# Linear attention followed by a gated MLP, one core: early loads on two hardware queues, ss a pair later between zero matmuls, and batch 1's q transposed by TensorE

## The chip, the cores and the metric

The kernel runs on one core of a Trainium2 chip. The metric is the device time of one execution in microseconds. A kernel's time is the median of several runs.

## The reference

Eight batches of eight heads, 576 positions, head width 64, all in float32. Attention has no softmax: per head a 64x64 matrix is built from k and v, q is multiplied by it, and each row is normalised by its root mean square and scaled by `g_norm`. The heads are put side by side (4608 rows of 512), and a two-layer MLP with a sigmoid-approximated GELU follows.

```python
kv = np.einsum('bhsd,bhse->bhde', k, v)
out = np.einsum('bhsd,bhde->bhse', q, kv)
rms = np.sqrt(np.mean(out * out, axis=-1, keepdims=True) + 1e-06)
attn_out = out / rms * g_norm                      # 8, 8, 576, 64
x = attn_out.transpose(0, 2, 1, 3).reshape(4608, 512)
h = x @ moe_w_in                                   # 512 -> 2048
g = h * (1.0 / (1.0 + np.exp(-1.702 * h)))
out = g @ moe_w_out                                # 2048 -> 512
```

## The kernel before

All matmuls are in float16 with float32 sums. Heads are handled in four pairs (`c` = 0 to 3), two heads of 64 side by side on 128 partitions. For a pair, attention is: `kv` (the pair's 64x64 matrices, copied to `kvb`), a transposed q (`qT`), `out` (one matmul of `kvb` with `qT`, then a square `sq` on ScalarE), `ss` (a matmul with ones that sums the squares over a head, then `ln` and `rs` on ScalarE) and `apply` (VectorE multiplies the out tile by `g_col` and `rs` into `xT`). 512 of the 576 rows of a batch go through its own dense block; the last 64 of all batches are gathered in `x_rem` for a ninth block.

`dense(t, ...)` is the MLP for 512 rows: 16 hidden tiles `hT` of four matmuls each with `w_in_sb`, a gate on ScalarE into `gT`, and 64 projection steps with `w_out_sb` into four `o` tiles, which are copied to `osb` and stored. Blocks 0 and 1 start with a group of four hidden tiles, for which the outer loop runs over the four parts `ko` of x. In block 0 the projection goes through the weights in four quarters (`deep`). Work of the next batch's attention is put between the matmuls of a block by two tables: `at1(i, f)` runs f after hidden tile i (or ahead of part i of the group), `at2(n, f)` after projection step n. Each engine executes in the order in which the code is written.

Batches 0 and 1 are loaded with 96 partitions of 6 rows each (`PE_`, `NJ`), the other batches with 128 partitions of 4 rows, whole and early by `load_batch`. Loads that GpSimd issues (`early_load`, `load_w_in`, `load_w_out`) go through one software queue and cast to float16 on the way; SyncE's and ScalarE's go through hardware queues and do not cast. Batch 0 (`First`): q and k of pairs 0 and 1 come by SyncE as float32 (`first`) and are cast by ScalarE and VectorE, everything else of it by GpSimd. Its q is transposed by TensorE through `ident` (12 transposes a pair). Batch 1 (`Second`): its q, k and v are packed into `qbuf` and `kbuf` by VectorE, and q is transposed by one DMA (`qTe`) that SyncE issues. Batches 2 to 7 use DMA transposes too (`qTd`, `qTr`). Batch 2's load is issued by `third`, which waits until `w_out` is complete.

Ahead of and between batch 0's matmuls stand zero matmuls: `busy(n)` multiplies a cleared tile n times into `idle_ps`, which nothing reads.

PSUM is divided into three pools: `ps_a` ("att", three buffers: out, ss, kvp), `ps_h` ("hT", three) and `ps_o` ("o", two).

Of the kernel before, what the change touches and what calls it, by code (L numbers as in the profile page):

```python
# [7 lines left out]
F16 = mybir.dt.float16  # L8
F32 = mybir.dt.float32
# [3 lines left out]
P = 128  # L13
# [3 lines left out]
def kernel(  # L17
# [10 lines left out]
    nc = tc.nc  # L28

    B, H, S, D = q.shape  # L30
    DM = H * D
    DFF = moe_w_in.shape[1]
    NPAIR = H // 2
# [3 lines left out]
    SM = 512  # L37
# [5 lines left out]
    PE_ = 96  # L43
    NJ = S // PE_
# [37 lines left out]
    def early_src(n, b, c0, c1):  # L82
        return srcs[n][b, 2 * c0 : 2 * c1].rearrange("h (p j) d -> p h (j d)", j=NJ)

    def early_load(n, b, c0, c1):
        nc.gpsimd.dma_start(
            out=raw[n][0:PE_, c0:c1, :].rearrange("p c (l x) -> p (c l) x", l=2),
            in_=early_src(n, b, c0, c1),
        )

    def pack(n, dst, c):

        nc.vector.tensor_copy(  # L93
            out=dst[0:PE_, c * NJ * P : (c + 1) * NJ * P].rearrange(
                "p (j l d) -> p j l d", j=NJ, l=2
            ),
            in_=raw[n][0:PE_, c, :].rearrange("p (l j d) -> p j l d", l=2, j=NJ),
        )
# [37 lines left out]
            nc.gpsimd.tensor_copy(out=t.rearrange("p c (l d) -> p (c l) d", l=2), in_=src[n])  # L136


    HW = 2
    first = {}  # L140
    for n in "qk":
        first[n] = stage.tile([P, H, J * D], F32, name=f"{n}f", tag=f"{n}f")
        first[n] = first[n].rearrange("p h x -> p (h x)")[0:PE_, 0 : HW * 2 * NJ * D]
        first[n] = first[n].rearrange("p (c x) -> p c x", c=HW)
    for c in range(HW):
        for n in "qk":
            nc.sync.dma_start(  # L147
                out=first[n][:, c, :].rearrange("p (h x) -> p h x", h=2),
                in_=early_src(n, 0, c, c + 1),
            )  # L150
    g_row = const.tile([1, D], F32)
    nc.scalar.dma_start(out=g_row, in_=g_norm.unsqueeze(0))
    nc.vector.memset(ident, 0.0)
    nc.vector.memset(kvb[1], 0.0)
    for c in range(HW):
        early_load("v", 0, c, c + 1)
    nc.gpsimd.affine_select(
        out=ident,
        in_=ident,
# [3 lines left out]
        pattern=[[-1, P]],  # L163
        channel_multiplier=1,
    )
    for c in range(HW, NPAIR):
        for n in "qkv":
            early_load(n, 0, c, c + 1)

    nc.scalar.preload_act_table_set("natural_log_exp_and_others")  # L170
# [8 lines left out]
    def load_w_in(f0, f1):  # L179
        nc.gpsimd.dma_start(  # L180
            out=w_in_sb[:, :, f0 * P : f1 * P],
            in_=moe_w_in[:, f0 * P : f1 * P].rearrange("(ko ki) f -> ki ko f", ki=P),
        )
# [8 lines left out]
    xT = {}  # L192

    class Attention:
        def __init__(self, b):
            self.b, self.kb = b, kvb[b % 2]
            self.qT, self.o = {}, {}
            self.x = xT[b] = xpool.tile([P, KO, SM], F16, name="xT", tag="xT")
# [23 lines left out]
        def transpose_q(self):  # L222
            s = attn.tile([P, NPAIR * J, P], F16, name="qTd", tag="qTd", bufs=1)
            nc.sync.dma_start_transpose(out=s, in_=qbuf[:, 0 : NPAIR * SM])
            self.qTr = attn.tile([P, 2, P], F16, name="qTr", tag="qTr", bufs=1)
            nc.sync.dma_start_transpose(
                out=self.qTr, in_=qrem[self.b % 2].rearrange("p c e -> p (c e)")
            )
            s = s.rearrange("p (c j) r -> p c (j r)", c=NPAIR)
            for c in range(NPAIR):  # L230
                self.qT[c] = s[:, c, :]
# [30 lines left out]
        def ss(self, c, table=False):  # L262
            if table:
                nc.scalar.preload_act_table_set("natural_log_exp_and_others")  # L264
            o, sq, n = self.o[c]
            t = ps_a.tile([P, SM], F32, name="ss", tag="att")
            nc.tensor.matmul(t[:, 0:n], ones2, sq[:, 0:n], start=True, stop=True)  # L267
            ln = attn.tile([P, SM], F32, name="ln", tag="ln", bufs=2)
            nc.scalar.activation(ln[:, 0:n], t[:, 0:n], AFT.Ln, bias=eps_t, scale=1.0 / D)  # L269
            rs = attn.tile([P, SM], F32, name="rs", tag="rs", bufs=2)  # L270
            nc.scalar.activation(rs[:, 0:n], ln[:, 0:n], AFT.Exp, bias=0.0, scale=-0.5)  # L271
            self.o[c] = (o, rs, n)
# [16 lines left out]

    class First(Attention):  # L290


        def kv(self, c):
            t = ps_o.tile([P, D], F32, name="kv0", tag="o")
# [16 lines left out]
        def q(self, c):  # L311
            t = ps_h.tile([P, S], F16, name="q0", tag="hT")
            for j in range(NJ):
                for hl in range(2):
                    nc.tensor.transpose(
                        t[hl * D : (hl + 1) * D, j * PE_ : (j + 1) * PE_],
                        qraw[0:PE_, c, (hl * NJ + j) * D : (hl * NJ + j + 1) * D],
                        ident[0:PE_, 0:PE_],
                    )
            s = attn.tile([P, S], F16, name="qT", tag="qT", bufs=4)  # L320
            nc.vector.tensor_copy(s, t)
            self.qT[c] = s
# [4 lines left out]
    class Second(Attention):  # L327


        def pack_q(self):  # L330
            for c in range(NPAIR):
                pack("q", qbuf, c)

        def pack_k(self, c):
            pack("k", kbuf, c)
# [14 lines left out]
            if c == NPAIR - 1:  # L350
                self.keep_kv()

        def transpose_q(self):
            s = attn.tile([P, NPAIR * NJ, PE_], F16, name="qTe", tag="qTe", bufs=1)
            nc.sync.dma_start_transpose(out=s, in_=qbuf[0:PE_, :])
            s = s.rearrange("p (c j) r -> p c (j r)", c=NPAIR)
            for c in range(NPAIR):
                self.qT[c] = s[:, c, 0:SM]
            self.qTe = s

        def rest(self, c):
            return self.qTe[:, c, SM:S]


    def dense(t, units1, units2, group, deep):
# [88 lines left out]

    a0 = First(0)

    def first_cast(c):
        nc.scalar.copy(qraw[0:PE_, c, :], first["q"][:, c, :])
        nc.vector.tensor_copy(kraw[0:PE_, c, :], first["k"][:, c, :])


    idle_ps = ps_h.tile([P, SM], F32, name="idle", tag="hT")
# [1 line left out]
    def busy(n):  # L464
        for _ in range(n):
            nc.tensor.matmul(
                idle_ps,
                kvb[1][:, 0, :],
                kvb[1].rearrange("p c r -> p (c r)"),
                start=True,  # L470
                stop=True,
            )

    first_cast(0)
    busy(8)
    g_ps = ps_o.tile([P, 1], F32, name="g_ps", tag="o")
    for hl in range(2):
        r = slice(hl * D, (hl + 1) * D)
        nc.tensor.matmul(g_ps[r, :], g_row, one_t, start=True, stop=True)
    nc.vector.tensor_copy(g_col, g_ps)  # L480
    a0.q(0)
    busy(6)
    first_cast(1)
    for c in range(NPAIR):
        last = c == NPAIR - 1
        a0.kv(c)
        if not last:
            a0.q(c + 1)
            if c:
                a0.apply(c - 1)  # L490
        a0.out(c)
        if last:
            a0.apply(c - 1)
        else:
            a0.ss(c)
            busy(1)
    load_w_in(0, 4)
    load_w_in(4, 8)
    load_w_in(8, 16)
# [20 lines left out]
    for t in range(NT):  # L520
        b = t + 1
        u1, u2 = {}, {}

        def at1(i, f, *args):
            u1.setdefault(i, []).append(lambda: f(*args))

        def at2(i, f, *args):
            u2.setdefault(i, []).append(lambda: f(*args))

        def of(b, name, *args):  # L530
            return lambda: getattr(live[b], name)(*args)

        if t == 0:
            at1(("ko", 1), of(0, "ss", NPAIR - 1))
            at1(("ko", 1), of(0, "apply", NPAIR - 1))
            at1(4, of(0, "out", NPAIR))
            at2(4, of(0, "ss", NPAIR, True))
            at2(4, of(0, "apply", NPAIR))
            at1(8, start, 1)
            for r in krem + vrem:  # L540
                at1(8, nc.vector.memset, r[R:P], 0.0)
            at1(12, of(1, "pack_q"))
            at1(12, of(1, "transpose_q"))
            for c in range(NPAIR):
                at2(12, of(1, "pack_k", c))
                at2(23 + c, of(1, "kv", c))
                at2(30 + 8 * c, of(1, "out", c))
                at2(38 + 8 * c, of(1, "ss", c))
                at2(38 + 8 * c, of(1, "apply", c))
            at2(14, third)  # L550
        elif b < B:
            if t == 1:
                at2(46, of(1, "out", NPAIR))
                at2(53, of(1, "ss", NPAIR))
                at2(53, of(1, "apply", NPAIR))
            f0 = 7 if t == 1 else 2
            at1(f0, casts, b)
            at1(f0, start, b)
            at1(f0, of(b, "transpose_q"))
            if t == 1:  # L560
                at1(f0, load_batch, 3)
            for c in range(NPAIR):
                at1((11 if t == 1 else 9) + c, of(b, "kv", c))
            for c in range(NPAIR + 1):
                at2(1 + 9 * c, of(b, "out", c))
                at2(8 + 9 * c, of(b, "ss", c, c == 0))
                at2(8 + 9 * c, of(b, "apply", c))
            if b + 2 < B:
                at2(2, load_batch, b + 2)
        dense(t, u1, u2, 4 if t < 2 else 0, t == 0)  # L570
# [30 lines left out]
```

## Time and profile before

| | before |
|---|---|
| median of 3 runs | 305.53 us (305.33 to 306.51) |
| profiled execution, its own time | 305.53 us |
| span of the profile | 303.7 us |
| granted TensorE clock, mean | 0.967 |
| TensorE busy | 289.4 us (95%), 1517 matmuls |
| ScalarE busy | 176.4 us (58%) |
| VectorE busy | 89.1 us (29%) |
| software queue | 7.14 MB written, 14.7% of 16 engines' span |
| hardware queue of SyncE | 35.99 MB, 40.6% |

The page of a profile divides the span into 40 slices and shows the busy share of each engine, the granted clock and the share of the DMA engines in tenths. The chain of work that ended last follows each step back to what released it. In the timeline a row has start, length, engine, line, operation, output<-inputs, and in brackets the idle time before it and what ended that. A row of the DMA issues gives the size of a transfer and the time from issue to landing. A row of a queue's table gives packets, MB and the share of 16 engines' time.

### The profile page before, as it was taken

Reading aid. Unit: us, or ns where it says so; the run is one execution under the profiler, and the core shown is the slowest. Engines: PE = TensorE matmul, PEld = TensorE weight load, DVE = VectorE, ACT = ScalarE, POOL = GpSimd, SP = SyncE. Lnnn points to the kernel's source line nnn. Section 1 sums busy time; section 2 is a strip of 40 time slices with the busy share of each in tenths; the row PEclk is TensorE's granted clock in tenths of the full one; section 3 lists DMA queues with packets and bytes.
Section 4 is the critical chain, followed back from the end, with each engine's and each line's share of the span. In section 5 each row is a group of like instructions: output and inputs, shape, how many; then the busy total and the mean of one; then the engine's idle time right before and its main releaser. Section 6 shows DMA issues by size and latency. Waiting matters only on the chain.

```text
span 303.7 us, 3828 instructions
## 1 busy us (share of the span) xinstructions
PE 289.4 (95%) x1517; PEld 134.2 (44%) x1517; DVE 89.1 (29%) x190; ACT 176.4 (58%) x284; POOL 22.8 (7%) x41
## 2 busy tenths in 40 slices
PE   7589997999999999999999999999999999999993
PEld 2234453445444544454445444544454444444441
DVE  2333030561455134413451245124612400110020
ACT  2458723886766685668566856686658657016400
POOL 7350000020210010001000200000000000000000
PEclk9758997999999999999999999999999999999998
DMA  7999995989997930794079407000700030002032
GB/s 174 205 210 206 194 175 151 361 189 339 337 333 146 369 92 2 220 345 120 1 217 332 136 0 216 2 0 2 217 0 0 2 138 0 2 35 105 0 71 69
DMA packets 56199, 43.38 MB, mean 143 GB/s; under 512 B 27252, under 2 KB 53364, under 8 KB 55412
## 3 DMA queue, kind: packets, MB, share of 16 engines
q1 hardware_dynamic: 48482, 35.99, 40.6%
q0 software_dynamic: 7696, 7.14, 14.7%
q8 instruction: 12, 0.20, 0.3%
q14 instruction: 7, 0.06, 0.1%
q10 hardware_dynamic: 2, 0.00, 0.0%
HBM read 36.70 MB, written 9.44 MB: 152 GB/s over the span
## 4 chain that ended last, share of the span: by engine, by line
PE 83%; DMA 12%; ACT 2%; DVE 1%; issue 0%; SPq 0%
PE o L411 39%; PE hT L370 35%; DMA qTe<-qbuf 6%; DMA qraw<-in_q_dram 3%; PE ss L267 3%; PE outT L239 3%; DMA kf<-in_k_dram 3%; PE kvp L205 2%; ACT sq L259 1%; ACT ln L269 0%; PE kvp L213 0%; ACT L379 0%; SPq L147 0%; ACT rs L271 0%; DVE qbuf L93 0%
## 5 line engine op out<-in xcount | busy, mean ns | idle before, releaser
L411 PE MATMUL o<-w_out_sb,gT 128*128 128x512 f16 x576 | 138.1, 382 | 0.0
L379 ACT ACTIVATE gT<-hT 128x512 f16<-128x512 f32 x142 | 84.5, 598 | 68.6 <-PE hT L370 68.5
L370 PE MATMUL hT<-xT,w_in_sb 128*128 128x512 f16 x504 | 116.8, 382 | 0.2 <-ACT gT L379 0.2
L411 PEld LDWEIGHTS <-gT 128*128 128x128 f16 x576 | 56.1, 98 | 66.6 <-issue 3.5
L370 PEld LDWEIGHTS <-w_in_sb 128*128 128x128 f16 x576 | 55.7, 99 | 63.8 <-issue 3.2
L277 DVE SCALAR_TENSOR_TENSOR xT<-outT,g_col,rs 128x512 f16<-128x512 f32 x32 | 24.0, 751 | 68.2 <-ACT rs L271 68.2
L419 DVE COPY osb<-o 128x512 f32<-128x512 f32 x34 | 23.3, 685 | 60.8 <-PE o L411 60.8
L269 ACT ACTIVATE ln<-ss,eps_t 128x512 f32<-128x512 f32 (+1 forms) x40 | 25.8, 645 | 21.0 <-PE ss L267 20.9
L259 ACT ACTIVATE sq<-outT 128x512 f16<-128x512 f32 (+1 forms) x40 | 21.7, 543 | 11.6 <-PE outT L239 11.3
L271 ACT ACTIVATE rs<-ln 128x512 f32<-128x512 f32 (+1 forms) x40 | 23.5, 587 | 1.3
L220 DVE CAST kvb<-kvp 64x256 f16<-64x256 f32 x14 | 5.9, 422 | 47.8 <-PE kvp L213 44.8
L267 PE MATMUL ss<-sq,ones 128*128 128x512 f16 (+1 forms) x40 | 15.4, 385 | 2.1 <-ACT sq L259 2.1
L370 PE MATMUL hT<-x_rem,w_in_sb 128*128 128x512 f16 x64 | 14.0, 379 | 0.0
L136 POOL CAST krem<-krf 64x512 f16<-64x512 f32 x6 | 3.6, 607 | 115.6 <-DMA krf<-in_k_dram 76.8
L379 ACT ACT_TABLE_LOAD x8 | 10.3, 1283 | 0.1
L131 DVE CAST qbuf<-qf 128x512 f16<-128x512 f32 x24 | 10.0, 481 | 0.0
L205 PEld LDWEIGHTS <-kbuf 128*128 128x128 f16 x96 | 7.4, 98 | 5.7
L281 DVE SCALAR_TENSOR_TENSOR x_rem<-outT,g_col,rs 128x256 f16<-128x256 f32 x8 | 3.9, 484 | 18.6 <-ACT rs L271 18.6
L205 PE MATMUL kvp<-vbuf,kbuf 128*128 128x128 f16 x96 | 9.3, 219 | 0.0
L239 PE MATMUL outT<-qTd,kvb 128*128 128x512 f16 x24 | 9.1, 379 | 0.0
L264 ACT ACT_TABLE_LOAD x7 | 9.0, 1283 | 0.1
L131 DVE CAST kbuf<-kf 128x512 f16<-128x512 f32 x24 | 8.8, 428 | 0.0
(54 smaller groups left out, 89.1 us busy)
## 6 DMA issues: line engine op xcount, KB each, us to landing
kf<-in_k_dram SPq DMA_DIRECT2D x6, 1024.0 KB, 5.8
vf<-in_v_dram SPq DMA_DIRECT2D x6, 1024.0 KB, 7.8
qf<-in_q_dram SPq DMA_DIRECT2D x6, 1024.0 KB, 10.6
out_dram<-osb SPq DMA_DIRECT2D x6, 1024.0 KB, 4.2
out_dram<-osb SPq DMA_DIRECT2D x12, 128.0 KB, 2.3
out_dram<-osb SPq DMA_DIRECT2D x6, 192.0 KB, 2.5
w_in_sb<-in_moe_w_in_dram POOLq DMA_DIRECT2D x2, 512.0 KB, 9.3
w_in_sb<-in_moe_w_in_dram POOLq DMA_DIRECT2D x1, 1024.0 KB, 13.7
```

Of the source, the lines that this page charges most:

```text
L131: nc.vector.tensor_copy(out=dst[:, c, :, :].rearrange("p j (l d) -> p j l d", l=2), in_=src[n][:, h, :].rearrange("p l (j d) -> p j l d", ...
L205: nc.tensor.matmul(t[:, c, :].rearrange("p (l d) -> p l d", l=2), kh[:, c, j, :], vh[:, 2 * c : 2 * c + 2, j * D : (j + 1) * D], start=(j ...
L239: nc.tensor.matmul(t.rearrange("p c r -> p (c r)"), self.kb[:, c, :], self.qT[c][:, 0:SM], start=True, stop=True,)
L259: nc.scalar.activation(sq[:, 0:n], t, AFT.Square)
L267: nc.tensor.matmul(t[:, 0:n], ones2, sq[:, 0:n], start=True, stop=True)
L269: nc.scalar.activation(ln[:, 0:n], t[:, 0:n], AFT.Ln, bias=eps_t, scale=1.0 / D)
L271: nc.scalar.activation(rs[:, 0:n], ln[:, 0:n], AFT.Exp, bias=0.0, scale=-0.5)
L277: nc.vector.scalar_tensor_tensor(self.x[:, c, :], o, g_col, rs, op0=ALU.mult, op1=ALU.mult)
L370: nc.tensor.matmul(h, w_in_sb[:, ko, fo * P : (fo + 1) * P], x[:, ko, :], start=(ko == 0), stop=(ko == KO - 1),)
L379: nc.scalar.activation(gT[:, fo, :], h, AFT.Gelu_apprx_sigmoid)
L411: nc.tensor.matmul(os[mo], gT[:, fo, mo * P : (mo + 1) * P], w_out_sb[:, fo, :], start=(fo == 0), stop=(fo == FO - 1),)
L419: (nc.scalar.copy if deep and mo % 2 else nc.vector.tensor_copy)(osb[:, mo, :], os[mo])
```

## The change

Three parts.

First, the early loads: k and v of pair 0 go on SyncE's hardware queue, q on ScalarE's, all as float32 with a cast on an engine (v's is new, on VectorE). Pair 1's q, k and v move to GpSimd's software queue, q ahead of the building of `ident`.

Second, the order of batch 0's attention: `ss` and `apply` follow one pair later, `q` of the next pair comes after `out`, and zero matmuls stand ahead of `out` (two), at the end of a pair (one) and ahead of the last `ss` (two). The whole of attention now ends ahead of the first hidden matmul; before, the last pair's `ss` and `apply` stood in block 0's group. Batch 0's `ss` tiles for the four pairs use the "o" buffers.

Third, batch 1's q: no DMA transpose; six TensorE transposes a pair after projection steps 9, 12, 15 and 18 of block 0, into an "att" tile that VectorE copies to `qT`.

```diff
-    HW = 2
     first = {}
-    for n in "qk":
+    for n, queue in (("k", nc.sync), ("q", nc.scalar), ("v", nc.sync)):
         first[n] = stage.tile([P, H, J * D], F32, name=f"{n}f", tag=f"{n}f")
...
-    for c in range(HW):
-        for n in "qk":
-            nc.sync.dma_start(
-                out=first[n][:, c, :].rearrange("p (h x) -> p h x", h=2),
-                in_=early_src(n, 0, c, c + 1),
-            )
+        queue.dma_start(
+            out=first[n].rearrange("p (h x) -> p h x", h=2), in_=early_src(n, 0, 0, 1)
+        )
...
-    for c in range(HW):
-        early_load("v", 0, c, c + 1)
+    early_load("q", 0, 1, 2)
     nc.gpsimd.affine_select(
...
-    for c in range(HW, NPAIR):
-        for n in "qkv":
+    for c in range(1, NPAIR):
+        for n in "qkv"[c == 1 :]:
             early_load(n, 0, c, c + 1)
...
+        ss_pool = (ps_a, "att")                    # Attention; First: (ps_o, "o")
...
-            t = ps_a.tile([P, SM], F32, name="ss", tag="att")
+            pool, tag = self.ss_pool
+            t = pool.tile([P, SM], F32, name="ss", tag=tag)
...
-        def transpose_q(self):
-            s = attn.tile([P, NPAIR * NJ, PE_], F16, name="qTe", tag="qTe", bufs=1)
-            nc.sync.dma_start_transpose(out=s, in_=qbuf[0:PE_, :])
...
+        def q(self, c):
+            t = ps_a.tile([P, S], F16, name="q1", tag="att")
+            for j in range(NJ):
+                nc.tensor.transpose(
+                    t[:, j * PE_ : (j + 1) * PE_],
+                    qbuf[0:PE_, (c * NJ + j) * P : (c * NJ + j + 1) * P],
+                    ident[0:PE_, 0:PE_],
+                )
+            s = attn.tile([P, S], F16, name="qT", tag="qT", bufs=4)
+            nc.vector.tensor_copy(s, t)
+            self.qT[c] = s
...
-    def first_cast(c):
-        nc.scalar.copy(qraw[0:PE_, c, :], first["q"][:, c, :])
-        nc.vector.tensor_copy(kraw[0:PE_, c, :], first["k"][:, c, :])
+    nc.scalar.copy(qraw[0:PE_, 0, :], first["q"])
+    nc.vector.tensor_copy(kraw[0:PE_, 0, :], first["k"])
+    nc.vector.tensor_copy(vbuf[0:PE_, 0, :], first["v"])
...
-    first_cast(0)
-    busy(8)
+    busy(12)
...
     a0.q(0)
-    busy(6)
-    first_cast(1)
+    busy(2)
     for c in range(NPAIR):
-        last = c == NPAIR - 1
         a0.kv(c)
-        if not last:
-            a0.q(c + 1)
-            if c:
-                a0.apply(c - 1)
-        a0.out(c)
-        if last:
-            a0.apply(c - 1)
-        else:
-            a0.ss(c)
+        busy(2)
+        a0.out(c)
+        if c:
+            a0.ss(c - 1)
+        if c > 1:
+            a0.apply(c - 2)
+        if c + 1 < NPAIR:
+            a0.q(c + 1)
             busy(1)
+    busy(2)
+    a0.ss(NPAIR - 1)
+    a0.apply(NPAIR - 2)
+    a0.apply(NPAIR - 1)
...
-            at1(("ko", 1), of(0, "ss", NPAIR - 1))
-            at1(("ko", 1), of(0, "apply", NPAIR - 1))
             at1(4, of(0, "out", NPAIR))
+            at2(4, setattr, a0, "ss_pool", Attention.ss_pool)
...
-            at1(12, of(1, "pack_q"))
-            at1(12, of(1, "transpose_q"))
             for c in range(NPAIR):
+                at1(12, of(1, "pack_q", c))
+                at2(9 + 3 * c, of(1, "q", c))
```

TensorE at the end of batch 0's attention, before: the last pair's out, then the hidden tiles of block 0 with the last ss among them (LDWEIGHTS rows load the stationary operand of the matmul below them).

```order
L239 LDWEIGHTS kvb_84
L239 MATMUL outT<-qT,kvb_84 128x512
L370 LDWEIGHTS w_in_sb
L370 MATMUL hT<-xT,w_in_sb 128x512
L370 LDWEIGHTS w_in_sb
L370 MATMUL hT<-xT,w_in_sb 128x512
L370 LDWEIGHTS w_in_sb
L370 MATMUL hT<-xT,w_in_sb 128x512
L370 LDWEIGHTS w_in_sb
L370 MATMUL hO<-xT,w_in_sb 128x512
L267 LDWEIGHTS ones_98
L267 MATMUL ss<-sq,ones_98 128x512
```

And the same place now:

```order
L235 LDWEIGHTS kvb_84
L235 MATMUL outT<-qT,kvb_84 128x512
L264 LDWEIGHTS ones_98
L264 MATMUL ss<-sq,ones_98 128x512
L468 LDWEIGHTS kvb_85
L468 MATMUL idle<-kvb_85 128x512
L468 LDWEIGHTS kvb_85
L468 MATMUL idle<-kvb_85 128x512
L264 LDWEIGHTS ones_98
L264 MATMUL ss<-sq,ones_98 128x512
L372 LDWEIGHTS w_in_sb
L372 MATMUL hT<-xT,w_in_sb 128x512
```

The first ss now is pair 2's, the second pair 3's; between them stand two zero matmuls (`idle`), and the hidden tiles follow after both.

VectorE in block 0's projection, before: from batch 0's last apply to the copy of batch 1's kv (`x4` is four such instructions in a row).

```order
L93 COPY qbuf<-qraw 96x768 x4
L281 SCALAR_TENSOR_TENSOR x_rem<-outT,g_col,rs 128x4x64
L93 COPY kbuf<-kraw 96x768 x4
L220 CAST kvb_85<-kvp 64x4x64 x2
L277 SCALAR_TENSOR_TENSOR xT<-outT,g_col,rs 128x512 x2
```

And now:

```order
L93 COPY qbuf<-qraw 96x768 x4
L278 SCALAR_TENSOR_TENSOR x_rem<-outT,g_col,rs 128x4x64
L360 COPY qT<-q_474 128x576
L93 COPY kbuf<-kraw 96x768
L360 COPY qT<-q_488 128x576
L93 COPY kbuf<-kraw 96x768 x3
L360 COPY qT<-q_518 128x576
L360 COPY qT<-q_530 128x576
L216 CAST kvb_85<-kvp 64x4x64 x2
```

Four copies of transposed q have come in, the second of them behind the first pack of k, all ahead of the copy of kv.

GpSimd at the start, before: v of pairs 0 and 1 go ahead of the select that builds `ident`, then pair 2 follows.

```order
L86 DMA vbuf<-in_v_dram 96x2x384 x2
L157 ISA
L157 AFFINE_SELECT ident<-ident 128x128
L86 DMA qraw<-in_q_dram 96x2x384
L86 DMA kraw<-in_k_dram 96x2x384
L86 DMA vbuf<-in_v_dram 96x2x384
```

And now:

```order
L86 DMA qraw<-in_q_dram 96x2x384
L151 ISA
L151 AFFINE_SELECT ident<-ident 128x128
L86 DMA kraw<-in_k_dram 96x2x384
L86 DMA vbuf<-in_v_dram 96x2x384
```

The first load on the software queue is pair 1's q, and pair 1's k and v stand behind the select, ahead of pairs 2 and 3, which are as before: nine loads instead of eight.

More of the change, by code (lines that the diff above doesn't have):

```diff
@@ L136, in casts @@
             nc.gpsimd.tensor_copy(out=t.rearrange("p c (l d) -> p (c l) d", l=2), in_=src[n])
-    HW = 2
     first = {}
-    for n in "qk":
+    for n, queue in (("k", nc.sync), ("q", nc.scalar), ("v", nc.sync)):
         first[n] = stage.tile([P, H, J * D], F32, name=f"{n}f", tag=f"{n}f")
-        first[n] = first[n].rearrange("p h x -> p (h x)")[0:PE_, 0 : HW * 2 * NJ * D]
-        first[n] = first[n].rearrange("p (c x) -> p c x", c=HW)
-    for c in range(HW):
-        for n in "qk":
-            nc.sync.dma_start(
-                out=first[n][:, c, :].rearrange("p (h x) -> p h x", h=2),
-                in_=early_src(n, 0, c, c + 1),
-            )
+        first[n] = first[n].rearrange("p h x -> p (h x)")[0:PE_, 0 : 2 * NJ * D]
+        queue.dma_start(
+            out=first[n].rearrange("p (h x) -> p h x", h=2), in_=early_src(n, 0, 0, 1)
+        )
     g_row = const.tile([1, D], F32)
@@ L290 @@
     class First(Attention):
+        ss_pool = (ps_o, "o")
         def kv(self, c):
@@ L327, with pack_q @@
     class Second(Attention):
-        def pack_q(self):
-            for c in range(NPAIR):
-                pack("q", qbuf, c)
+        def pack_q(self, c):
+            pack("q", qbuf, c)
         def pack_k(self, c):
@@ L351, in kv @@
                 self.keep_kv()
-        def transpose_q(self):
-            s = attn.tile([P, NPAIR * NJ, PE_], F16, name="qTe", tag="qTe", bufs=1)
-            nc.sync.dma_start_transpose(out=s, in_=qbuf[0:PE_, :])
[L356 to L359, printed above, removed]
+        def q(self, c):
[9 more added lines that the diff above has]
+            self.qT[c] = s
         def rest(self, c):
-            return self.qTe[:, c, SM:S]
+            return self.qT[c][:, SM:S]
     def dense(t, units1, units2, group, deep):
```

## The prediction

> **What bounds the kernel now.** I read first the page's head and its slices, then the chain of work that ended last, then the stretches where its clock row dips.
>
> ```profile
> span 303.7 us, 3828 instructions
> PE 289.4 (95%) x1517; PEld 134.2 (44%) x1517; DVE 89.1 (29%) x190; ACT 176.4 (58%) x284; POOL 22.8 (7%) x41
> PEclk9758997999999999999999999999999999999998
> DMA  7999995989997930794079407000700030002032
> ```
>
> TensorE is busy 95% of the span, so only its gaps and its slow stretches can give time. The granted clock is below full in slices 2 to 4 (7.6 to 30 us) and 7 (45.6 to 53 us); the DMA engines are full until slice 6 and have gaps only much later. The chain says the same from the other side:
>
> ```profile
> 28.38 18.74 DMA qTe<-qbuf
> 47.26 0.38 PE outT L239
> ...
> 61.84 7.07 PE hT L370 x32
> ```
>
> Up to 47.26 us the chain runs through attention of batch 0, a load of batch 1's q and its DMA transpose (18.74 us from issue to landing). From 61.84 us to the last copy it is TensorE throughout. Whatever the change does, it does before 61.84 us; later work is the same and should only shift. The stretches of half a microsecond place the clock's steps (second column: length; PE busy; then, after POOL, the clock):
>
> ```profile
> 10.50:11.00 0.50, 0.25 (x1) 0.13 (x2) 0.50 (x2) 0.00 (x0) 0.47 (x2) 0.72 1.30 197
> 24.00:24.50 0.50, 0.50 (x3) 0.21 (x2) 0.08 (x1) 0.48 (x2) 0.00 (x0) 0.62 1.33 207
> ...
> 48.00:48.50 0.50, 0.50 (x4) 0.21 (x3) 0.00 (x0) 0.27 (x1) 0.02 (x1) 0.77 0.00 0
> 51.50:52.00 0.50, 0.50 (x4) 0.15 (x3) 0.00 (x0) 0.50 (x1) 0.00 (x0) 0.82 1.08 385
> ```
>
> A mean of 0.72 of which the rest is 0.50 means a drop at 10.72; in the same way the clock is back at 24.38, drops at 48.27 and is back at 51.68. So there are two cold stretches, 13.7 and 3.41 us long, in which TensorE does half.
>
> **Part 1: the early loads and the first matmuls.** What follows attention is batch 0's dense block: 64 matmuls into the hidden tiles, then 64 projection steps. How early can the projection start?
>
> ```profile
> 18.52 0.89 POOL L186 DMA_DIRECT2D w_out_sb<-in_moe_w_out_dram  x1
> w_out_sb<-in_moe_w_out_dram POOLq DMA_DIRECT2D x1, 1024.0 KB, 14.0
> w_in_sb<-in_moe_w_in_dram POOLq DMA_DIRECT2D x1, 1024.0 KB, 13.7
> 9.74 1.82 POOL L180 DMA_DIRECT2D w_in_sb<-in_moe_w_in_dram  x2 [1.25 <-DMA vbuf<-in_v_dram]
> 7.73 0.76 POOL L180 DMA_DIRECT2D w_in_sb<-in_moe_w_in_dram  x1 [0.95 <-DMA vbuf<-in_v_dram]
> w_in_sb<-in_moe_w_in_dram POOLq DMA_DIRECT2D x2, 512.0 KB, 9.3
> 36.85 1.24 PE L411 MATMUL o<-w_out_sb,gT 128*128 128x512 f16 x5
> ```
>
> Its first weights land at 18.52 + 14.0 = 32.5 us, but the projection starts at 36.85: 4.3 us are lost to late compute. The weights of the hidden tiles land at about 17.0, 19.1 and (issued at 10.8, the second of the pair at 9.74) 24.5 us. So once compute is early enough, supply on the one software queue sets the start. That supply moves a little:
>
> ```profile
> q1 hardware_dynamic: 351, 0.51, 94.4%
> q0 software_dynamic: 2, 0.00, 0.7%
> ...
> q0 software_dynamic: 389, 0.28, 56.9%
> q1 hardware_dynamic: 358, 0.51, 43.4%
> ...
> q0 software_dynamic: 561, 0.40, 130.7%
> ```
>
> These are queue tables of 2 to 3.7, 4 to 8 and 10 to 12 us. Until 3.7 us the software queue moves nothing and the hardware queue 206 packets a us; while both run they manage (389 + 358) / 4 = 187 together; the software queue alone, 280. The change has three hardware and nine software loads where there were four and eight, 2304 data packets both ways. In the old order both queues run from 3.7 to about 9 us; in the new one pair 0's 576 packets leave after 3.7 us some 225, done with as many of the other queue at about 6.1 us. Some 3 us less of mixing at 187 instead of 280 is worth 1.0 us; I take 0.9 (bounds 0 and 1.2). Hence w_in at 16.1, 18.2, 23.6, w_out's first half at 31.6.
>
> The Trainium skill, "DMA: Bandwidth & Descriptors", section "Issuing engines are not separate DMA queues", says that issuing from several engines saves only the time to initiate, since all share the same 16 DMA engines. By that rule the 0.9 would be 0 and the forecast 0.9 later; the trace agrees with the sharing, but its 187 against 280 packets speaks for a small gain from less mixing.
>
> Can compute follow? Pair 0's kv waits for v:
>
> ```profile
> 4.67 0.45 PE L315 MATMUL q<-ident,qraw 96*64 96x96 f16 x12
> 5.05 1.47 PE L466 MATMUL idle<-kvb 128*128 128x512 f16 x6
> 7.49 0.38 PE L298 MATMUL kv<-vbuf,kraw 96*64 96x64 f16 x12 [0.96 <-DMA vbuf<-in_v_dram]
> 9.55 0.45 PE L315 MATMUL q<-ident,qraw 96*64 96x96 f16 x12 [1.69 <-ACT qraw L458]
> L315 PE MATMUL q<-ident,qraw 96*64 96x96 f16 x48 | 2.2, 244 | 1.7 <-ACT qraw L458 1.7
> L459 DVE CAST kraw<-kf 96x768 f16<-96x768 f32 x2 | 1.1, 556 | 7.2 <-DMA kf<-in_k_dram 7.2
> 6.14 0.64 POOL L86 DMA_DIRECT2D vbuf<-in_v_dram  x1
> vbuf<-in_v_dram POOLq DMA_DIRECT2D x4, 144.0 KB, 7.6
> ```
>
> v now lands at about 7.0 (its packets done near 6.1, and some time to be seen) and has a cast of 0.56 on VectorE, one more than before, behind k's, so kv starts near 7.6, no earlier than today. The difference comes after: there is no wait for pair 1's ScalarE cast (1.69), and ss follows a pair later, when sq is done. A pair costs TensorE at full clock about 0.38 (kv) + 0.22 (out) + 0.22 (ss) + 0.38 (q) + 3 x 0.22 (zero matmuls) = 1.9 us. Pair 3's v, last of the nine software loads, lands at 6.14 + 7.6 = 13.7 today and 0.9 less then, and kv, two zero matmuls, out, ss, two more and the last ss end at about 15. The first hidden matmul then waits for w_in at 16.1. The ScalarE chain sq, ln, rs of the last two pairs ends near 17.5, its table load (1.28) near 18.8; both lie beside the first 16 hidden matmuls (3.5 us). Tiles 8 to 15 wait for w_in at 23.6 and end, 8 x 0.864 later, at 30.6; then w_out at 31.6 decides. Compute has 1 us to spare, and a start up to 17 us costs nothing. If the clock falls at 7.4 for one period of 3.4 us, 1.7 us are lost and 0.3 to 0.7 of them show. The start moves from 36.85 to 31.6: **-5.25** (bounds: 0 and -6.2, with w_out as early as the tiles end).
>
> The queues that steps are moved past: q's load on ScalarE's queue stands ahead of the table load, which is due only at the first sq; on GpSimd pair 1's q goes ahead of the identity's select and k, v and the rest behind it, and the ninth load waits in issue for the first to land near 7, long before the queue gets to it. With ss in the "o" buffers, each takes one whose reader (a kvb multiply, a ln) ended a pair ago. The 10 extra zero matmuls stand in gaps that DMA sets; uncovered, at half clock, they cost 0.43 each, 4.3 us, which belongs to rival A.
>
> **Part 2: batch 1's q on TensorE.**
>
> ```profile
> 42.13 0.50 PE L343 MATMUL kvp<-vbuf,kbuf 96*128 96x128 f16 x6
> 42.47 0.38 PE L411 MATMUL o<-w_out_sb,gT 128*128 128x512 f16 x1
> 42.69 0.50 PE L343 MATMUL kvp<-vbuf,kbuf 96*128 96x128 f16 x6
> 47.26 0.38 PE L239 MATMUL outT<-qTe,kvb 128*128 128x512 f16 x1 [2.09 <-DMA qTe<-qbuf]
> ```
>
> Removed: the wait of 2.09 us: **-2.09**. The cold stretch that starts 1 us after it lasts 3.41 us and did half the work: **-1.7**. What could be late next is the kvb copy (0.86, in VectorE's idle time); in the new order two qT copies are ahead of it, done by projection step 20 of the 26 that precede it.
>
> Added: 24 transposes with 128-column weights and 96 moving columns. Nearest row: six kvp matmuls with the same 96x128 weights take 42.47 - 42.13 = 0.34 us; four times that is 1.4, a little less with 96 columns instead of 128. I take **+1.2** (bounds: 1.0, by columns, and 24 x 244 ns = 5.9 if none overlapped). Four VectorE copies of about 0.45 lie where VectorE idles. The second of them stands behind a kbuf copy that waits for k (34.5); who waits for it is the kvp tile, which takes its buffer at step 23 (37.9).
>
> Batch 1's k and v must not be late. Their supply without the DMA transpose:
>
> ```profile
> q0 software_dynamic: 932, 0.82, 127.6%
> ...
> q0 software_dynamic: 1274, 1.02, 90.9%
> q1 hardware_dynamic: 1274, 0.33, 34.9%
> vbuf<-in_v_dram POOLq DMA_DIRECT2D x1, 576.0 KB, 19.8
> 20.94 0.77 POOL L86 DMA_DIRECT2D vbuf<-in_v_dram  x1
> ```
>
> From 24 to 28 us the software queue writes 0.82 / 4 = 205 GB/s; from 33 to 40, beside the transpose, 146. At 205, k lands at 34.5 and v at 37.3 (today 20.94 + 19.8 = 40.7), the rest of w_out at 39.9 and 42.4. kv is due at step 23: 31.6 + 23 x 0.216 + 1.3 = 37.9. It is close, but covered. Batch 2's load starts when w_out is complete, 5.4 us earlier than today against 7.8 for TensorE; its casts would begin near 54.8, and batch 2's kv near 61: covered.
>
> **Sum.** The profiled execution took 305.53 us, 1.83 outside its span, and equals the median of the runs. 305.53 - 5.25 - 2.09 - 1.7 + 1.2 = 297.7.
>
> **Rivals.**
> A. The clock stays at half through attention. For it: it did so from 10.72 to 24.38, though TensorE was about three quarters busy. Against: the zero matmuls fill the gaps, and one full period, 21 to 24.4, brought it back. Four pairs at 3.2 us from 7.6 put the hidden tiles at 20.2 and, with their cold start, the projection near 35.9: 302.0.
> B. The software queue stays at 146 GB/s after 32 us: v lands at 39.8, kv waits 1.9, batch 2 another 0.4: 300.0. Against: the 256-byte transposes alone share those stretches.
> C. Transposes do not overlap: 24 x 244 ns, +4.7: 302.3. Against: twelve L315 transposes and the next matmul are 0.38 us apart. The Trainium skill, "TensorE: Matmul & The Clock Gate", "Part 4: PE-mode transpose", gives about 275 ns for one in a kernel and says that they do not count for the clock; by that figure, 6.6 us, an estimate.
> D. The new queues do not bring supply forward, w_out stays at 32.5: 298.6.
> E. Slower: hidden tiles run at half clock throughout, because waits for w_in break every period. The 64 cost 0.43 instead of 0.216 each and end at 16.1 + 27.6 = 43.7, 6.9 after today's start of the projection: with part 2, 309.8. It decides from 39.4 on (36.85 + 2.6). Against: supply of four hidden tiles takes 2.6 us, their matmuls 3.5.
>
> **How the numbers follow.** Forecast 0.59, A 0.10, B 0.13, C 0.05, D 0.10, E 0.03. The range leaves out A, C and E (0.18): below, 296.3, with the earlier start of part 1 and cheapest transposes; above, 301.0, past B. Half a per cent (1.5 us) is what a measurement can tell from no change; only E, and a tail of A and C (0.03), lie above 304.0. Faster 0.94, same 0.03, slower 0.03.
>
> **What would show it.** The first projection step near 31.6, waiting for w_out; no wait at batch 1's out, and full clock from 45 to 55; 24 transposes in about 1.2 us; the first hidden matmul of the second block's second group near 54. A late first hidden matmul at half clock would mean A; a wait on v at kv, B.

## The result, and the profile after

The changed kernel takes 297.63 us (median of 4 runs, 297.12 to 298.06) against 306.02 us before (4 runs): a ratio of 0.9726, 95% interval 0.9696 to 0.9757. The forecast was 297.7. The profiled execution took 297.12 us, 8.41 less than the one before. The head of its page:

```profile
span 295.4 us, 3904 instructions
PE 286.7 (97%) x1551; PEld 134.2 (45%) x1551; DVE 90.4 (31%) x194; ACT 175.1 (59%) x283; POOL 23.6 (8%) x42
PEclk9999999999999999999999999999999999999999
DMA  8999969889988906870489034001600030021033
```

Both cold stretches are gone: no slice is below 9 tenths of the clock. The chain of work that ended last, at the places quoted of before:

```profile
13.99 16.82 DMA w_out_sb<-in_moe_w_out_dram
...
40.31 0.39 PE outT L235
...
53.36 7.07 PE hT L372 x32
```

The long DMA in it is now w_out's first half, and from its landing at 30.8 us on TensorE, VectorE's short copy of kv and ScalarE carry the chain. TensorE's timeline at the waits that are left:

```profile
16.09 0.82 PE L372 MATMUL hT<-xT,w_in_sb 128*128 128x512 f16 x3 [0.98 <-DMA w_in_sb<-in_moe_w_in_dram]
30.86 1.25 PE L413 MATMUL o<-w_out_sb,gT 128*128 128x512 f16 x5 [0.47 <-DMA w_out_sb<-in_moe_w_out_dram]
33.13 0.42 PE L354 MATMUL q<-ident,qbuf 96*128 96x96 f16 x6
33.39 0.81 PE L413 MATMUL o<-w_out_sb,gT 128*128 128x512 f16 x3
40.31 0.39 PE L235 MATMUL outT<-qT,kvb 128*128 128x512 f16 x1
```

The hidden tiles start when w_in lands, the projection when w_out does, and batch 1's out no longer waits for q: in the chain it follows VectorE's copy of kv. The budget against before, up to the second block's second group (the row of 32 `hT`, 61.84, now 53.36): start of the projection 36.85 to 30.86, -5.99; the wait for the DMA transpose, -2.09; from projection to out, 9.45 against 8.32 without that wait, +1.13; from out to the second group, 13.05 against 14.58, -1.53. That is -8.48; the rest of the span is the same to 0.2.

### The profile page after: what moved, and what is told of

Same layout as the page of the kernel before. It is cut to its first block, busy times and chain, and to the rows that moved or that the text cites. A ratio compares the mean times of both kernels' runs of the same rounds, so it can differ in the third digit from the quotient of the medians.

```text
span 295.4 us, 3904 instructions
## 1 busy us (share of the span) xinstructions
PE 286.7 (97%) x1551; PEld 134.2 (45%) x1551; DVE 90.4 (31%) x194; ACT 175.1 (59%) x283; POOL 23.6 (8%) x42
## 3 DMA queue, kind: packets, MB, share of 16 engines
HBM read 36.70 MB, written 9.44 MB: 156 GB/s over the span
## 4 chain that ended last, share of the span: by engine, by line
PE 87%; DMA 7%; ACT 3%; DVE 1%; issue 0%; POOL 0%
PE o L413 41%; PE hT L372 36%; DMA w_out_sb<-in_moe_w_out_dram 6%; PE ss L264 3%; PE outT L235 2%; PE kvp L201 2%; DMA qf<-in_q_dram 2%; PE idle L468 1%; ACT ln L266 0%; PE kvp L341 0%; PE kvp L209 0%; ACT L381 0%; ACT rs L268 0%; PE q L314 0%; ACT sq L255 0%
## 5 line engine op out<-in xcount | busy, mean ns | idle before, releaser
L372 PE MATMUL hT<-xT,w_in_sb 128*128 128x512 f16 x504 | 115.4, 379 | 1.2 <-DMA w_in_sb<-in_moe_w_in_dram 1.0
L413 PEld LDWEIGHTS <-gT 128*128 128x128 f16 x576 | 55.5, 98 | 65.4 <-issue 2.0
L264 PE MATMUL ss<-sq,ones 128*128 128x512 f16 (+1 forms) x40 | 14.3, 357 | 0.0
L131 DVE CAST qbuf<-qf 128x512 f16<-128x512 f32 x24 | 9.4, 453 | 2.5 <-DMA qf<-in_q_dram 2.5
L468 PE MATMUL idle<-kvb 128*128 128x512 f16 x27 | 8.9, 442 | 1.3 <-DVE kvb L149 1.3
```

What stands on the lines that cost most here:

```text
L131: nc.vector.tensor_copy(out=dst[:, c, :, :].rearrange("p j (l d) -> p j l d", l=2), in_=src[n][:, h, :].rearrange("p l (j d) -> p j l d", ...
L372: nc.tensor.matmul(h, w_in_sb[:, ko, fo * P : (fo + 1) * P], x[:, ko, :], start=(ko == 0), stop=(ko == KO - 1),)
L413: nc.tensor.matmul(os[mo], gT[:, fo, mo * P : (mo + 1) * P], w_out_sb[:, fo, :], start=(fo == 0), stop=(fo == FO - 1),)
```

## The experiments

Three groups of kernels, each group run on one chip beside the kernel before; ratios are to that kernel, with 95% intervals. The changed kernel measured 297.66 and 297.74 in the second and third group. The first group (each part alone, no zero matmuls, the first try of the old order) had no run of it; there 297.63, from the result, stands for it. The second group holds the old loads, the extra load and w_out first, the third the rest.

**Each part alone.** Batch 1's q by TensorE in the kernel before, the rest as it was:

```diff
...
-            at1(12, of(1, "pack_q"))
-            at1(12, of(1, "transpose_q"))
             for c in range(NPAIR):
+                at1(12, of(1, "pack_q", c))
+                at2(9 + 3 * c, of(1, "q", c))
```

> The kernel before with only batch 1's q transposed by TensorE; loads and order of batch 0 stay. Theory: the projection still starts at 36.85 us; 24 transposes cost 1.04 (0.26 for six, as the changed kernel shows), the wait of 2.09 goes and with it the cold stretch (1.5 to 1.7): 2.6 to 2.8 us faster than before, about 303.2. If the two parts were independent, this and part 1 alone would together give the 8.4 of both. Rival: the wait is only replaced by one for batch 1's k and v, no gain.

Measured: 302.41 us (before on the same chip: 305.04), ratio 0.9895 (0.9844 to 0.9946). The two places in its timeline:

```profile
36.17 1.24 PE L414 MATMUL o<-w_out_sb,gT 128*128 128x512 f16 x5
45.61 0.39 PE L239 MATMUL outT<-qT,kvb 128*128 128x512 f16 x1
```

From projection to out are 9.44 us without a wait, as in the changed kernel. The gain is 2.6 us, as expected.

The other part alone: loads and order new, the DMA transpose put back.

```diff
...
+            at1(12, of(1, "pack_q"))
+            at1(12, of(1, "transpose_q"))
             for c in range(NPAIR):
-                at1(12, of(1, "pack_q", c))
-                at2(9 + 3 * c, of(1, "q", c))
```

> The changed kernel with the DMA transpose of batch 1's q put back. Theory: the projection starts at 30.8, but batch 1's q lands at 25.8 and its transpose takes some 18.7 us beside the software queue, so batch 1's first out comes at 45 to 46 instead of 47.26: the wait grows from 2.1 to about 6.5 us, the clock falls again, and only 1 to 2 us of the 6 are kept: about 304.5. Rival (independent parts): the wait stays 2.1, 5.7 us faster than before, 299.8.

Measured: 303.41 us, ratio 0.9942 (0.9913 to 0.9970), 1.6 us faster than before.

```profile
31.51 1.25 PE L410 MATMUL o<-w_out_sb,gT 128*128 128x512 f16 x5 [0.84 <-DMA w_out_sb<-in_moe_w_out_dram]
41.14 0.49 PE L342 MATMUL kvp<-vbuf,kbuf 96*128 96x128 f16 x6 [4.16 <-DMA vbuf<-in_v_dram]
46.73 0.38 PE L235 MATMUL outT<-qTe,kvb 128*128 128x512 f16 x1 [1.01 <-DMA qTe<-qbuf]
```

The projection starts 5.3 us earlier than before, but batch 1's out only 0.5: the waits between them are 5.2 us, where before they were 2.1. The size was expected, the place only in part: most of the wait is for batch 1's v, which lands at 41.1 beside the DMA transpose (at 37.0 in the changed kernel of the second group), and only 1.0 is for the transpose itself. What is kept lies mostly behind out: the clock falls ahead of it here (from 42.4 to 45.8), and from out to the second group are 13.0 us instead of 14.58. The queue tables from 33 to 40 us, this kernel's two rows first, then the one of the changed kernel in the second group:

```profile
q0 software_dynamic: 1060, 0.86, 90.6%
q1 hardware_dynamic: 1058, 0.27, 42.8%
...
q0 software_dynamic: 1607, 1.43, 126.6%
```

Beside the transpose the software queue writes 0.86 MB in 7 us (123 GB/s), without it 1.43 (204). So the parts are not independent: alone they give 2.6 and 1.6 us, together about 8. The transposes on TensorE give alone about what their terms in the budget add up to (2.5); the early start gives most of its gain only once the DMA transpose is gone.

**What in the first part counts.** The changed kernel without the 13 zero matmuls in and after the pairs:

```diff
         a0.kv(c)
-        busy(2)
         a0.out(c)
...
-            busy(1)
-    busy(2)
     a0.ss(NPAIR - 1)
```

> The changed kernel without the zero matmuls in and after the pairs (13 fewer; the 14 ahead of them stay). Theory: pairs still end by the time that w_in lands (16.1), but TensorE is about half busy, the clock falls in this stretch and the hidden tiles start cold: up to 1.7 us lost, of which 0.5 are covered by the wait for w_out: 0.5 to 1.5 us slower than the changed kernel, 298.1 to 299.1. Rival: the DMA supply decides alone and the zeros do nothing: 297.6. Rival: the clock stays low through all hidden tiles: 302 or more.

Measured: 298.12 us (297.24, 297.42, 298.81, 299.23), ratio 0.9743 (0.9683 to 0.9804). The profiled run is the slowest of them; its clock rows and the start of the hidden tiles and the projection:

```profile
14.50:15.00 0.50, 0.33 (x1) 0.00 (x0) 0.00 (x0) 0.50 (x2) 0.50 (x2) 0.72 1.19 195
21.50:22.00 0.50, 0.50 (x4) 0.20 (x3) 0.00 (x0) 0.13 (x1) 0.00 (x0) 0.95 1.10 200
...
16.26 1.46 PE L372 MATMUL hT<-xT,w_in_sb 128*128 128x512 f16 x3 [1.01 <-DMA w_in_sb<-in_moe_w_in_dram]
32.99 1.24 PE L413 MATMUL o<-w_out_sb,gT 128*128 128x512 f16 x5
```

Here the clock was down from 14.7 to 21.5, through most of the first hidden group, and the projection started 2 us later. Two runs show no loss at all. By its median the loss is 0.5 us against 297.63, at the lower end of the expected range; the runs differ by more than that, so the size is not settled.

The old order of batch 0's attention with the new loads, run twice:

```diff
+        last = c == NPAIR - 1
         a0.kv(c)
-        busy(2)
+        if not last:
+            a0.q(c + 1)
...
         a0.out(c)
-        if c:
-            a0.ss(c - 1)
...
+        if last:
+            a0.apply(c - 1)
+        else:
+            a0.ss(c)
             busy(1)
...
```

> The changed kernel with the old order of batch 0's attention (ss in the same pair, one zero matmul a pair, the last ss and apply in block 0's group); the new loads and TensorE's transposes of batch 1's q stay. Theory: each pair waits for sq and the clock falls as before, so the first hidden matmul comes at 16.5 to 18 and at half clock; the projection starts at 32.5 to 34 instead of 30.86: 299.3 to 300.8. Rival: the loads alone make the gain, 297.6.

> The kernel with the old order of the first group again, with more runs: three of its four runs were at 297.6, one, the profiled one, at 298.8 with the clock down from 11.4 to 18. Theory: when the clock falls, it costs 1.1 us, and this differs between runs by the phase of the clock's periods: median 297.7 to 298.8, spread over 1 us. Rival: the order is worth nothing, and 298.8 was one disturbed run: all at 297.6.

Measured: 297.67 us (four runs, 297.64 to 298.78), ratio 0.9747 (0.9698 to 0.9796), and 297.69 (six runs, 297.16 to 298.70), ratio 0.9753 (0.9717 to 0.9789). The changed kernel in the latter group: 297.74, 297.34 to 297.89. The first expectation missed: by the median the order is worth nothing with the new loads. The second held: one of these four runs and two of the six are 1 us slower, at a granted clock of 0.984 against 0.995 to 1.000 in the seven others, and none of the changed kernel's sixteen runs is. The last profile, of a run of 297.76, shows how the old order keeps up:

```profile
15.07 0.81 PE L371 MATMUL hT<-xT,w_in_sb 128*128 128x512 f16 x3
31.48 1.25 PE L412 MATMUL o<-w_out_sb,gT 128*128 128x512 f16 x5 [0.83 <-DMA w_out_sb<-in_moe_w_out_dram]
```

The hidden tiles start even earlier than in the changed kernel, the clock stayed at full, and w_out sets the projection again. In the profiled run of the first try (298.78) the clock was down from 11.3 to 18.1, and the projection came at 32.55 without a wait for w_out.

Old order and no zero matmuls in the pairs (the cut is against the old order):

```diff
         else:
             a0.ss(c)
-            busy(1)
```

> The changed kernel with the old order of batch 0's attention and no zero matmuls in the pairs (13 fewer): new loads and TensorE's transposes alone. Theory: attention ends within 1 us of the landing of w_in, the clock falls, hidden tiles run at half clock for 2 to 5 us, of which the wait for w_out covers 0.5: 298.1 to 299.6. Rival: order and zeros are worth nothing here, 297.6.

Measured: 298.62 us (297.50 to 299.13), ratio 0.9775 (0.9734 to 0.9815), 0.9 more than the changed kernel, as expected, though the intervals overlap, and again a spread of 1.6 us where the changed kernel has 0.6. Order and zero matmuls together buy this 0.9 and the narrow spread. By the medians the old order with its zero matmuls loses nothing and the new order without them 0.5, but neither has the narrow spread (1.1, 1.5 and 2.0 us). Why the clock falls in some runs and not in others no run here shows.

The old loads with the new order:

```diff
-    for n, queue in (("k", nc.sync), ("q", nc.scalar), ("v", nc.sync)):
+    for n in "qk":
...
-    early_load("q", 0, 1, 2)
+    for c in range(HW):
+        early_load("v", 0, c, c + 1)
...
+    first_cast(1)
```

> The changed kernel with the early loads as they were (q and k of pairs 0 and 1 on SyncE's queue, v on the software queue), the new order and TensorE's transposes kept. Theory: supply of w_in and w_out comes 0.9 to 1.7 us later and nothing else decides: projection at 31.8 to 32.5, 298.5 to 299.3. Rival (the same 16 DMA engines move the same bytes): no difference, 297.6. Rival: pair 1's casts and late q delay attention and the clock falls: 300 or more.

Measured: 301.34 us, ratio 0.9847 (0.9805 to 0.9888), 3.7 more than the changed kernel: over twice what the supply alone should cost. VectorE and TensorE in its profile (a run of 299.80, so one that lost less than most; four of the six were above 301):

```profile
9.68 0.56 DVE L467 CAST kraw<-kf 96x768 f16<-96x768 f32 x1 [1.75 <-DMA kf<-in_k_dram]
10.15 0.28 DVE L310 TENSOR_TENSOR kvb<-kv,ones 128x128 f16<-128x128 f32 x1
10.49 0.52 PE L241 MATMUL outT<-qT,kvb 128*128 128x512 f16 x1 [1.57 <-DVE kvb L310]
19.00 0.81 PE L378 MATMUL hT<-xT,w_in_sb 128*128 128x512 f16 x3
```

Pair 0's kv was done at 8.4, but its kvb multiply stands in VectorE's queue behind the cast of pair 1's k, which lands at 9.65. So pair 0's out waits for pair 1's load, and the clock falls at the end of the gap (down from 10.6 to 14.0). The kernel before has the same rows; there TensorE had already waited 1.69 us for ScalarE's cast of pair 1's q, and waits another 0.75 for kvb:

```profile
9.94 0.56 DVE L459 CAST kraw<-kf 96x768 f16<-96x768 f32 x1 [4.19 <-DMA kf<-in_k_dram]
10.41 0.28 DVE L305 TENSOR_TENSOR kvb<-kv,ones 128x128 f16<-128x128 f32 x1
10.75 0.61 PE L239 MATMUL outT<-qT,kvb 128*128 128x512 f16 x1 [0.75 <-DVE kvb L305]
```

To test that in the kernel with the old loads and the new order, only that cast was moved:

```diff
-    first_cast(1)
+    nc.scalar.copy(qraw[0:PE_, 1, :], first["q"][:, 1, :])
...
         a0.kv(c)
+        if c == 0:
+            nc.vector.tensor_copy(kraw[0:PE_, 1, :], first["k"][:, 1, :])
```

> The kernel with the old early loads of the second group, with one instruction moved: VectorE's cast of pair 1's k now stands behind pair 0's kvb multiply instead of ahead of it. Theory: with the old loads VectorE, in order, waits for k of pair 1 (9.65 us) ahead of kvb, so pair 0's out comes at 10.5 instead of 8.7, TensorE idles 1.6 us and the clock falls; moved, out comes at 8.5 to 8.8, the first hidden matmul at 16.5 to 17.2 instead of 19.0, and 1.5 to 2.8 of the 3.7 us come back: 298.5 to 299.8. What is left against the changed kernel is supply, 0.9 to 1.7. Rival: supply is the whole cost of the old loads, nothing changes, 301.3.

Measured: 298.02 us (297.88 to 299.33), ratio 0.9770 (0.9734 to 0.9806). One instruction moved back by one place gives 3.3 of the 3.7 us; more than expected. In its profile, taken on its slowest run:

```profile
8.93 0.29 DVE L310 TENSOR_TENSOR kvb<-kv,ones 128x128 f16<-128x128 f32 x1 [1.55 <-PE kv L303]
10.27 0.56 DVE L495 CAST kraw<-kf 96x768 f16<-96x768 f32 x1 [1.04 <-DMA kf<-in_k_dram]
17.22 0.82 PE L378 MATMUL hT<-xT,w_in_sb 128*128 128x512 f16 x3
33.12 1.25 PE L419 MATMUL o<-w_out_sb,gT 128*128 128x512 f16 x5 [0.95 <-DMA w_out_sb<-in_moe_w_out_dram]
```

kvb no longer waits for the cast, the clock stays at full, the hidden tiles start 1.8 us earlier, and the projection waits for w_out. What then is left of the old loads' cost is 0.3 us by the medians (298.02 against 297.74), less than the 0.9 to 1.7 expected.

**Does supply set the start?** One more load of 144 KB, which nothing reads, ahead of batch 1's q on the software queue:

```diff
     load_w_in(8, 16)
+    spare = const.tile([P, 2 * NJ * D], F16)
+    nc.gpsimd.dma_start(
+        out=spare[0:PE_, :].rearrange("p (l x) -> p l x", l=2), in_=early_src("v", 0, 0, 1)
+    )
```

> The changed kernel with one more load of 144 KB (read by nobody) on the software queue between the last of w_in and batch 1's q. Theory: supply of w_out sets the start of the projection, so it comes 147456 B / 205 GB/s = 0.72 us later and the kernel is 0.6 to 0.8 us slower than the changed one. Rival: TensorE's own work decides, under 0.2 us.

Measured: 298.54 us (297.90 to 298.70), ratio 0.9766 (0.9733 to 0.9800): +0.88 against the changed kernel in the group, a little over the 0.6 to 0.8 expected.

```profile
32.38 1.25 PE L413 MATMUL o<-w_out_sb,gT 128*128 128x512 f16 x5 [1.50 <-DMA w_out_sb<-in_moe_w_out_dram]
```

The hidden tiles end 0.4 us later than in the changed kernel's profile of the group (w_in landed later), and the wait for w_out grows by 1.0 on top of that. Supply sets the start.

The reverse, w_out's first quarter ahead of batch 1's q:

```diff
+    load_w_out(0, 4)
     early_load("q", 1, 0, 4)
-    load_w_out(0, 8)
+    load_w_out(4, 8)
```

> The changed kernel with the first quarter of w_out ahead of batch 1's q on the software queue. Theory: the wait of 0.47 us for w_out goes, nothing else waits (batch 1's q would land near 28.5, needed at 33): 0.4 to 0.5 us faster than the changed kernel, about 297.1. Rival: batch 1's q or the second quarter is late, or ScalarE's chain at the block's end takes it back: 0 or slower.

Measured: 297.33 us (296.81 to 297.38), ratio 0.9729 (0.9696 to 0.9762), against 297.66 (297.24 to 297.91; ratio 0.9744) for the changed kernel: 0.33 us less, the lowest time here, though the intervals overlap.

```profile
30.36 1.24 PE L413 MATMUL o<-w_out_sb,gT 128*128 128x512 f16 x5
37.32 0.49 PE L341 MATMUL kvp<-vbuf,kbuf 96*128 96x128 f16 x6 [0.47 <-DMA vbuf<-in_v_dram]
```

The wait for w_out is gone, but a wait of 0.47 us for batch 1's v, a later load in the same queue, has come in: the expectation that nothing else waits missed.

## Why the prediction was right, point by point

**The number.** The forecast of 297.7 was met to 0.1 us, and that is partly luck. It took 7.8 us off 305.53; the change took off 8.4, and the kernel before measured 306.02 beside it. The terms were near, each in its place: the start 0.74 more than forecast, the others within 0.2.

**Start of the projection.** Right that w_out's landing sets it (the extra load shows it), a little low in size: -5.25 forecast, -5.99 measured; in the two later profiles of the changed kernel the start was at 30.96 and 31.41, so -5.4 to -6.0. The model of the supply, both kinds of queue sharing until 6.1 us, is not what happened. The queue tables of the changed kernel for 2 to 3.7, 3.7 to 4.9 and 7 to 10 us:

```profile
q1 hardware_dynamic: 161, 0.24, 46.2%
q10 hardware_dynamic: 129, 0.20, 35.5%
...
q1 hardware_dynamic: 182, 0.26, 80.0%
q10 hardware_dynamic: 81, 0.10, 27.3%
q0 software_dynamic: 6, 0.00, 2.5%
...
q0 software_dynamic: 842, 0.60, 130.6%
```

Up to 4.9 us the software queue moved next to nothing; from 5.5 us on it ran alone, at 842 / 3 = 281 packets a us, the rate forecast for it alone. The size of the term, 0.9, nevertheless holds by the bytes: up to 30 us the software queue had written 5.10 MB against 4.77 before, of which the ninth load is 0.15; the other 0.18 are 0.9 us at 205 GB/s (0.4 against the kernel with only batch 1's q changed, which had written 4.87). The landing of w_out scatters more than that: it comes at 30.8, 30.9 and 31.4 in the three profiles of the changed kernel, and at 32.5 and 32.1 in the two with the old loads and the old order. So the 1.7 between the first two profiles is not all supply. Rival D, which had w_out stay at 32.5, is refuted by these landings; yet by the medians the old loads with the cast moved cost only 0.3 us.

Compute had less to spare than the 1 us of the prediction. Tiles 8 to 15 did not wait for w_in: from 16.09 TensorE ran without a wait to about 30.4, and the wait for w_out was 0.47 to 0.82 us in the three profiles. A start at 17 would have cost some 0.1 to 0.4 us, by an estimate from these waits (0.9 later, less the wait).

**How compute keeps up.** The result was right (the last ss at 14.73, forecast 15), the reason given was incomplete. The step "kv starts near 7.6, no earlier than today. The difference comes after" named two things: the missing wait for ScalarE's cast of pair 1's q, 1.69 us on TensorE before, and the later ss. It passed over a third, VectorE's cast of pair 1's k ahead of pair 0's kvb, though the row was in the chain of before (a DMA of kf, then kvb). The new loads give pair 1 to the software queue, so neither cast exists any more. With the old loads and the new order the cast of k is worth 3.3 us. What the wait for ScalarE and the later ss are worth with the old loads no run isolates; the new order and its zero matmuls together are worth some 1.7 there (4.3 us under the kernel before with them and TensorE's transposes, 2.6 with the transposes alone, in different groups). With the new loads the old order does as well as the new one by the median. The kernel before with only that cast moved was not run.

**Batch 1's q.** The wait of 2.09 went in full. Six transposes stand 33.39 - 33.13 = 0.26 us ahead of the next step, 1.04 for 24 (forecast 1.2), and rival C, at 244 ns each, is refuted. The Trainium skill, "TensorE: Matmul & The Clock Gate", "Part 4: PE-mode transpose", has about 275 ns for one of 128x128 in a kernel; here, with 96 columns, they follow each other every 43 ns. The clock stayed at full from 31 to 36 us, with these 24 among the matmuls. The clock's term was -1.7 and came out at -1.53. ScalarE's chain from the last ss to the second group takes 6.08 us in both kernels, so the gain lies ahead of it; where the missing 0.17 went is open.

**Supply without the DMA transpose.** Rival B is refuted: 204 GB/s in the second group's profile from 33 to 40 us, as the 205 forecast, and kv had no wait.

**Clock.** Rivals A and E, a clock at half through attention or through the hidden tiles, did not occur in any of the three profiles of the changed kernel (mean granted clock 0.997 and 0.998).

## What to carry to other kernels

Before a start is put down to slow loads or a slow clock, look at what stands ahead of the late instruction on its own engine: a cast that waits for the next pair's load held this pair's work, and moving it one place was worth 3.3 us. An early start is worth no more than the next input allows: alone the two parts gave 1.6 and 2.6 us, together 8. Where one ordered queue feeds a stage, as here, the time saved on the engine ended where that queue's next load landed, and changing the order of the loads moved part of the wait to a later one.

## What the runs showed that was not expected

The software queue's first load was issued at 1.3 us in both kernels, but it moved next to nothing for some time: in the changed kernel 6 packets up to 4.9 us, when 53 of the hardware queues' 626 were left, and in the kernel before it began at about 3.6 us, with over half of the hardware queue's packets left. Why it waits is open. The two hardware queues together moved fewer packets from 2 to 3.7 us (161 + 129) than the one did before (351), because they got going later: from 3 to 3.5 us they moved 127, the one 117.

A DMA transpose of 0.6 MB holds up ordinary loads beside it by more than its bytes: in 7 us 1.43 MB of loads without it, with it 0.86 beside 0.27 of the transpose.
